# An attention and gated feed-forward block on one core: score and P·V half-steps regrouped in pairs of key blocks

## The chip, the cores and the metric

The kernel runs on one core of a Trainium2 chip. The metric is the device time in microseconds of one execution. Before the change three runs took 1682.72, 1683.56 and 1688.05 us; the median is 1683.56 us.

## What is computed

The reference is a transformer block with conditioned layer norms: 2048 rows of width 512, 32 query heads of width 16 on one shared key and value head, and a gated feed-forward part of inner width 1792.

```python
mod = (silu(c) @ w_mod).reshape(1, 6, 1, -1)          # sa, ca, ga, sb, cb, gb
h = layernorm(x) * (1 + ca) + sa
q, k, v = h @ wq (32 heads), h @ wk, h @ wv           # one k, one v for all heads
p = softmax(q k^T / 4)                                # per head, 2048 x 2048
x = x + ga * ((p v) @ wo)
h = layernorm(x) * (1 + cb) + sb
x = x + gb * ((sigmoid(h @ w_gate) * (h @ w_up)) @ w_down)
```

All products whose operands would lose too much in 16 bits are made of three passes with a high and a low part of each operand (`passes`, L470). P·V is done in float32.

## The kernel before

**Units and steps.** A prologue (the list `PLAN`, L38) makes the norms, k, v and the first q. Then a loop runs over 32 units (L1106): a unit is 256 query rows (`QU`) and 8 of the 32 heads. A unit has 16 steps `kb`, one for each block of 128 keys, and each step has two half-steps `n` (L1131). So there are 1024 half-steps.

**Halves of the array.** TensorE works as eight tiles of 64 rows by 32 columns: two halves by rows, called sides here, and four column strips. `columns` (L145) issues four matmuls, one for each strip of one side; they run together, since each has a tile of its own. A matmul's side follows from the partitions of its operands: partitions 0 to 63 are side 0, 64 to 127 side 1.

**What a half-step issues** is set by `ORDER` (L57): `a0, s0, c, a1, s1`, and then a piece of other work.
- `a` (`a_tile`, L603) is a tile of scores with queries on the partitions, into a bank `sa` (three banks). VectorE takes the maximum of each row (`a_max`, L597, line L136 in the profile, tile `mx`). These tiles run 84 ahead (`A0`), that is 21 steps.
- `s` (`st_tile`, L634) is a tile of scores with keys on the partitions, into a bank `st` (two banks); ScalarE takes its exponential into `P`.
- `c` (`pv`, L647) is P·V for a key block whose exponentials were made `LAG` = 2 steps ago: four matmuls of float32, one in each strip, each in two passes, so that eight show in the profile (`craw<-P,V`). They add to one PSUM bank `craw`, which both sides write in turn.

`sides(t)` (L578) gives the sides of the two half-steps of key block t: (0, 1) for even t and (1, 0) for odd t. In half-step `n` with `h = sides(kb)[n]`, the `a` and `s` tiles use side `1 - h`. `pv` uses side `sides(t)[n]` of its own key block `t = kb - 2`, which is as even or odd as `kb`.

**Turns.** When P·V passes from one side to the other, `hand_over` (L159) puts a tiny matmul behind the last one of the old side (`craw<-nought` in the profile), which counts up a semaphore, and `take_over` (L169) makes TensorE's queue wait for that count before the first P·V of the new side. Before the change `pv` hands over after the first half-step of each key block and takes over in its second.

**Pieces.** `piece` (L1095) puts a share of another product at the end of a half-step: q, the output projection (`po`), gate and up (`pgu`), down (`pd`), or a transposition (`pt`). Such a product is a `Couple` (L191) of two groups: each of its terms is a `columns` call on the side that P·V does not use and then one on the side that it does. `plan` and `places` (L1034, L1070) spread a group's terms over half-steps by rates (`RATE` 2.2 terms, fewer for some). `Transposes` (L785) are placed whole, and `split_evac` (L353) then writes the high and the low part of the norm's result: ScalarE scales it, VectorE casts the high part (`h2h`), GpSimd subtracts for the low part (`h2l`).

**Maxima.** When the last `a` tile of a unit is made (`n == 62`, L600), the next step gathers the maxima (`max_end`, L608, VectorE), its second half-step transposes them on TensorE and copies them on ScalarE (`max_rows`), and behind the first half-step of the step after that VectorE makes their low part and SyncE issues four small DMAs into two rows of the unit's `qp` tile (`low`, `qp<-mh`). The unit's `s` matmuls read these rows.

**Order.** All work of TensorE, VectorE and ScalarE in the loop is kept in the order of the program (`Ordered`, L130). After the loop, outside that order, come the last P·V, the last output projections and the last quarter of the feed-forward part (L1157 to L1191), with matmuls of 128 by 128.

Of the kernel before, what the change touches and what calls it, by code (L numbers as in the profile page):

```python
# [9 lines left out]
F32 = mybir.dt.float32  # L10
AF = mybir.ActivationFunctionType
ALU = mybir.AluOpType
# [4 lines left out]
P = 128  # L17
# [38 lines left out]
A0 = 84  # L56
ORDER = "a0", "s0", "c", "a1", "s1"  # L57
LAG = 2
# [31 lines left out]
def adaln_mqa_glu_kernel(  # L90
# [39 lines left out]
    class Ordered:  # L130
        def __init__(self, engine):
            self.engine = engine
# [36 lines left out]
    def take_over(since=None):  # L169
        pe.wait_ge(turn, done[0] if since is None else since)  # L170
# [20 lines left out]
    class Couple:  # L191
# [3 lines left out]
        def part(self, n0, n1):  # L195
            if n0 == 0:
                for g in self.gs:
                    g.open()
            m = self.gs[0].n
            for n in range(n0, n1):  # L200
                if n == m:
                    take_over(self.since)
                for j in (1 - side[0], side[0]):
                    g = self.gs[j ^ (n >= m)]
                    l_, r_, *cut = g.term(n % m, slice(64 * j, 64 * j + 64))
                    columns(cut[0](g.bank) if cut else g.bank, l_, r_, n == 0, n == 2 * m - 1)
                if n == m - 1:
                    self.since = None
                    if open_[0]:
                        hand_over()  # L210
                        self.since = done[0]
            if n1 == self.n:
                for k, g in enumerate(self.gs):
                    g.end(g.bank, k == 1)
# [138 lines left out]
    def split_evac(src, k, sc, sh, hi, lo):  # L353
        h32 = t32("h32")[:, :QU]
        act.activation(h32, src, AF.Identity, scale=sc[:, k:k + 1], bias=sh[:, k:k + 1])
        dve.tensor_copy(hi, h32)  # L356
        pool.tensor_tensor(lo, h32, hi, op=ALU.subtract)  # L357


# [216 lines left out]


    def sides(t):  # L578
        return (0, 1) if t % 2 == 0 else (1, 0)

    def spot(n):
        return n // 16, n // 8 % 2, n % 2, n // 2 % 4
# [14 lines left out]
    def a_max(i, n, sa):  # L597
        kc, qt, j, r = spot(n)
        dve.tensor_reduce(mxs[i][:, 4 * j + r, qt, kc:kc + 1], sa, axis=AX.X, op=ALU.max)
        if i > 0 and n == 62:  # L600
            pend.append((i,))

    def a_tile(i, n):  # L603
        a_max(*a_product(i, n))

    pend = []

    def max_end(i):  # L608
        m16 = wp.tile([64, 32], F32, tag="m16", name="m16", bufs=4)
# [24 lines left out]
    def st_tile(i, t, pr, j, second):  # L634
        qp = get_q(i)
        if not second:
            P_[pr] = P2.tile([P, 2, 512], F32, tag=f"P{pr}", name=f"P{pr}", bufs=PBUFS)
        p_ = P_[pr]
        s_ = sbank("st")
        columns(s_, kp[64 * j:64 * j + 64, t * P:(t + 1) * P], qp[64 * j:64 * j + 64, 2 * pr:2 * pr + 2].rearrange("p r q -> p (r q)"),  # L640
                True, True)
        act.activation(p_[:, j], s_, AF.Exp, scale=0.25)
        Ps[i, t, 2 * j + pr] = p_[:, j]
# [3 lines left out]
    def pv(i, t, second):  # L647
        c_ = raw_c["c"]
        side[0] = j = sides(t)[second]
        rs = slice(64 * j, 64 * j + 64)  # L650
        start, stop = t == 0 and not second, t == NKB - 1 and second
        if second:
            take_over()
        for hh in range(4):
            z = pe.matmul(c_[32 * hh:32 * hh + 32, :], V[rs, t, :], Ps[i, t, hh][rs, :], start=start, stop=stop)
            if start and hh == 0 and i > 0:
                behind(z, raw_c["out"])
        open_[0] = not stop
        if not second:
            hand_over()  # L660
        raw_c["last"] = z
        if second:
            for hh in range(4):
                del Ps[i, t, hh]
            if stop:
                unit_end(i)
# [118 lines left out]
    class Transposes:  # L785
        stage, n = "tr", 4

        def __init__(self, part, u):
            self.part, self.u = part, u

        def alone(self):
            self.part(0, 4)
# [1 line left out]
    def ffn_groups(b):  # L794
# [57 lines left out]
        def tr_part(u, z, n0, n1):  # L852
            if n0 == 0:
                pts2[z] = bank("pt2")
            pt = pts2[z]
            for n in range(n0, n1):
                k, t = 2 * z + n // 2, 2 * u + n % 2
                pe.transpose(pt[:, n * P:(n + 1) * P], x1[t][1][:, k * P:(k + 1) * P], ident)
            if n1 == 4:
                for k in range(2 * z, 2 * z + 2):  # L860
                    if u == 0:
                        h2[k] = t16("h2h"), t16("h2l")
                    split_evac(pt[:, k % 2 * QU:(k % 2 + 1) * QU], k, mods[4], mods[3],
                               *(h_[:, u * QU:(u + 1) * QU] for h_ in h2[k]))
# [82 lines left out]
            return Group("dn", 3 * n_, "pd", term, end)  # L947

        wos = [wo_group(t) for t in range(4)]
        trs = [Transposes(lambda n0, n1, u=u, z=z: tr_part(u, z, n0, n1), u) for z in range(2) for u in range(2)]  # L950
        gs = []
        at = len(uses) - NFC
        es = [Couple(gu_half(p, 0, 0, p), gu_half(p, 1, 0, p)) for p in range(0, ahead, 2)]
# [116 lines left out]
    def plan(s, hb):  # L1070
        if run:
            return
        g = pick(s)
        if g is None:
            lead[0] = 0.0
            return
        if g.stage == "tr":
            sizes = [4]
        else:
            q = g.stage == "q" and s < FIRST  # L1080
            light = not q and g.stage == "gu" and s < 2 * NU * NKB + SKIP
            rate, most = (QRATE, 1) if q else (ERATE, 2) if light else (RATE, MOST)
            sizes = []
            for leg in range(2):
                sizes += places(g.n // 2, hb + len(sizes), rate, most, (3 if leg == 0 else 0) if q else 0 if light else None, g.w)
            if hb + len(sizes) > 2 * len(units) * NKB:
                spare.insert(0, g)
                return
        at = 0
        for z in sizes:  # L1090
            run.append((g, at, at + z))
            at += z
        assert at == g.n, (at, g.n, g.stage)

    def piece(s, h):  # L1095
        plan(s, 2 * s + h)
        if run:
            g, n0, n1 = run.pop(0)
            if n1 > n0:
                g.part(n0, n1)  # L1100
# [5 lines left out]
    for i, (b, o) in enumerate(units):  # L1106
        if o == 0 and b == NQ - 1:
            ends = ffn_groups(NB - 1)
            first_rows.append(Couple(*ends[0][:2]))
        if o == 0 and b % 2 == 1 and b < NQ - 1:  # L1110
            blocks[b // 2] = ffn_groups(b // 2)
            wos, trs, _, es = blocks[b // 2]
            main.extend([*ready(b // 2, [Couple(*wos[:2]), trs[0], trs[2]], i), (None, len(es)), *ready(b // 2, es, i)])
        if o == 0 and b % 2 == 0 and b > 0:
            wos, trs, gs, _ = blocks.pop(b // 2 - 1)
            gs = [Couple(*wos[2:]), trs[1], trs[3], *gs]
            main.extend([*ready(b // 2 - 1, gs[:-KEPT], i), (None, KEPT), *ready(b // 2 - 1, gs[-KEPT:], i)])
        for kb in range(NKB):
            s = i * NKB + kb
            now[0] = s  # L1120
            if kb == NKB - QLEAD - 5 and i + 2 < len(units):
                get_q(i + 2)
            late, pend[:] = pend[:], []
            for z in [z for z in waits if z[0] <= s]:
                waits.remove(z)
                z[1]()
            rows = [max_end(*z) for z in late]
            an = A0 + 4 * s

            old, lows[:] = lows[:], []  # L1130
            for n, h in enumerate(sides(kb)):  # L1131
                for z in ORDER:
                    k = int(z[1:] or 0)
                    if z[0] == "a" and an + 2 * k + 1 - h < len(alist):
                        a_tile(*alist[an + 2 * k + 1 - h])
                    if z == "c" and len(vq) >= LAG:
                        pv(*vq[0], n == 1)
                    if z[0] == "s":
                        st_tile(i, kb, k, 1 - h, n == 1)
                if n == 1:  # L1140
                    lows.extend(z() for z in rows)
                piece(s, n)
                if n == 0:
                    for z in old:
                        z()
            if len(vq) >= LAG:
                vq.pop(0)
            vq.append((i, kb))
            while wdone < nw:
                if wdone < nw - 4 and (wdone + 0.5) * WSTEPS > (s + 1) * (nw - 4):  # L1150
                    break
                if wdone >= nw - 4 and s < WLAST + 3 * (wdone - nw + 4):
                    break
                wjobs[wdone]()
                wdone += 1
    assert wdone == nw and len(qdone) == 4 * NB
    while run:  # L1157
        piece(s, 1)
    while vq:
        for n in range(2):  # L1160
            pv(*vq[0], n == 1)
        vq.pop(0)
    while waits:
        now[0] += 1
        for z in [z for z in waits if z[0] <= now[0]]:
# [54 lines left out]
```

## Time and profile before

| | |
|---|---|
| median of three runs | 1683.56 us |
| the profiled execution's own time | 1685.55 us |
| its span, first to last instruction | 1683.7 us |
| TensorE (PE) busy | 1644.5 us, 98% |
| VectorE (DVE) busy | 1430.9 us, 85% |
| ScalarE (ACT) busy | 1295.4 us, 77% |
| GpSimd (POOL) busy | 610.5 us, 36% |
| mean granted TensorE clock | 0.99 |

PE's busy time counts a matmul from its start to its modelled end, and matmuls of different tiles and of the same pipeline overlap, so 98% does not say that the array is full. A row of a timeline gives start, length, engine, line, operation, tiles and count; neighbours of one kind are put together. `64*32` is the tile of the array that a matmul uses. L136 is a helper: everything that passes through `Ordered` has this line, so groups are told apart by their tiles.

### The profile page before, as it was taken

Reading aid. Unit: us, or ns where it says so; the run is one execution under the profiler, and the core shown is the slowest. Engines: PE = TensorE matmul, PEld = TensorE weight load, DVE = VectorE, ACT = ScalarE, POOL = GpSimd, SP = SyncE. Lnnn points to the kernel's source line nnn. Section 1 sums busy time; section 2 is a strip of 40 time slices with the busy share of each in tenths; the row PEclk is TensorE's granted clock in tenths of the full one; section 3 lists DMA queues with packets and bytes.
Section 4 is the critical chain, followed back from the end, with each engine's and each line's share of the span. In section 5 each row is a group of like instructions: output and inputs, shape, how many; then the busy total and the mean of one; then the engine's idle time right before and its main releaser. Section 6 shows DMA issues by size and latency. Waiting matters only on the chain.

```text
span 1683.7 us, 87854 instructions
## 1 busy us (share of the span) xinstructions
PE 1644.5 (98%) x39747; PEld 974.6 (58%) x39747; DVE 1430.9 (85%) x2428; ACT 1295.4 (77%) x2335; POOL 610.5 (36%) x784
## 2 busy tenths in 40 slices
PE   6999999999999999999999999999999999999998
PEld 3335445454456666666656666666666666654443
DVE  7789999999999999999999999999999999912311
ACT  5548889888888888888888888888888888884100
POOL 4432445475033442222543232223543333132423
PEclk9989999999999999999999999999999999999999
DMA  7111333331011120101021110100121110011211
GB/s 242 57 62 28 103 114 96 98 96 40 21 61 41 57 70 15 41 28 28 28 77 53 47 45 15 41 24 27 38 78 49 45 53 16 24 47 52 88 51 38
DMA packets 86722, 94.05 MB, mean 56 GB/s; under 512 B 24916, under 2 KB 65868, under 8 KB 86348
## 3 DMA queue, kind: packets, MB, share of 16 engines
q1 hardware_dynamic: 86348, 88.44, 17.0%
q8 instruction: 311, 5.10, 1.2%
q14 instruction: 63, 0.52, 0.1%
HBM read 67.82 MB, written 16.24 MB: 50 GB/s over the span
## 4 chain that ended last, share of the span: by engine, by line
PE 83%; DVE 11%; ACT 2%; issue 1%; DMA 1%; POOL 0%; SPq 0%; POOLq 0%; ACTq 0%; DVEq 0%
PE craw L136 23%; PE sa L136 16%; PE pgu L136 14%; PE st L136 10%; DVE mx L136 9%; PE pd L136 6%; PE pgu L187 5%; PE pd L187 3%; PE po L136 2%; PE pq L136 2%; ACT P L136 1%; DMA xall<-in_A_x_dram 1%; ACT th L136 1%; DVE h2h L136 1%; DVE st L136 1%
## 5 line engine op out<-in xcount | busy, mean ns | idle before, releaser
L136 DVE TENSOR_REDUCE mx<-sa 128x1 f32<-128x512 f32 x2048 | 1291.5, 682 | 64.0 <-PE sa L136 29.1
L136 ACT ACTIVATE P<-st 128x512 f32<-128x512 f32 x2048 | 1175.2, 598 | 197.2 <-PE st L136 133.6
L136 PE MATMUL craw<-P,V 64*32 64x512 f32 x8192 | 1088.0, 598 | 0.2
L136 PE MATMUL sa<-kp,qp 64*32 64x512 f16 (+1 forms) x7940 | 826.6, 378 | 10.5 <-DVE mx L136 9.8
L136 PE MATMUL st<-qp,kp 64*32 64x512 f16 x8192 | 831.8, 379 | 4.8 <-ACT P L136 4.5
L136 PEld LDWEIGHTS <-kp 64*32 64x32 f16 x8192 | 323.9, 91 | 254.5 <-issue 102.2
L136 PEld LDWEIGHTS <-qp 64*32 64x32 f16 (+1 forms) x7940 | 284.4, 92 | 166.5 <-issue 82.4
L136 PE MATMUL pgu<-h2h,gw 64*32 64x512 f16 x5248 | 273.8, 376 | 1.0
L136 PEld LDWEIGHTS <-gw 64*32 64x32 f16 x7872 | 175.0, 92 | 59.4 <-issue 16.2
L136 PEld LDWEIGHTS craw<-P,V 64*32 64x32 f32 x8192 | 184.5, 105 | 15.0 <-issue 2.0
L136 PE MATMUL pgu<-h2l,gw 64*32 64x512 f16 x2624 | 165.3, 376 | 0.3 <-POOL h2l L357 0.3
L901 POOL TENSOR_SCALAR th<-th 128x512 f32<-128x512 f32 x41 | 25.4, 620 | 356.0 <-ACT th L136 300.2
L136 PE MATMUL craw<-nought 64*32 64x1 f16 x571 | 93.1, 163 | 0.0
L557 POOL MEMSET qp<- 32x1024 f16 x60 | 56.7, 945 | 83.3 <-PE st L136 80.8
L321 POOL TENSOR_SCALAR wst<-wst 128x512 f32<-128x512 f32 x46 | 28.5, 621 | 144.7 <-DMA wst<-in_B_w_up_dram 89.4
L187 PE MATMUL pgu<-h2h,gw 128*128 128x512 f16 x240 | 71.9, 379 | 1.5 <-DVE h2h L356 1.5
L136 PEld LDWEIGHTS <-nought 64*32 64x32 f16 x571 | 53.1, 93 | 34.2 <-issue 28.8
L895 ACT ACTIVATE th<-pgu 128x512 f32<-128x512 f32 x15 | 9.0, 597 | 82.1 <-PE pgu L187 82.1
L136 PE MATMUL pd<-wdh,gh 64*32 64x512 f16 x1152 | 70.4, 376 | 0.6 <-DVE t L136 0.2
L136 PE MATMUL pd<-wdl,gh 64*32 64x512 f16 x1152 | 70.3, 376 | 0.0
L136 PE MATMUL pd<-wdh,gl 64*32 64x512 f16 x1152 | 69.7, 376 | 0.0
L136 DVE COPY u<-pgu 128x512 f32<-128x512 f32 x41 | 28.0, 682 | 48.6 <-PE pgu L136 48.4
(160 smaller groups left out, 1426.8 us busy)
## 6 DMA issues: line engine op xcount, KB each, us to landing
gw<-wD SPq DMA_DIRECT2D x56, 512.0 KB
wD<-gw SPq DMA_DIRECT2D x14, 512.0 KB
wm<-in_w_mod_dram SPq DMA_DIRECT2D x6, 1024.0 KB
qp<-qD SPq DMA_DIRECT2D x192, 32.0 KB
qD<-q SPq DMA_DIRECT2D x16, 256.0 KB
xr<-in_A_x_dram SPq DMA_DIRECT2D x16, 256.0 KB
out_dram<-ot SPq DMA_DIRECT2D x16, 256.0 KB
raw<-cs SPq DMA_DIRECT2D x248, 16.0 KB
```

The lines of the kernel that those rows point to most:

```text
L136: return (lambda *a, **k: keep(f_(*a, **k))) if pinned else f_
L187: pe.matmul(cut[0](self.bank) if cut else self.bank, l_, r_, start=(n == 0), stop=(n == self.n - 1))
L321: pool.tensor_scalar(w_, w_, SW, 0.0, op0=ALU.mult, op1=ALU.add)
L557: eng.memset(qp[j:j + 32], 0.0)
L895: act.activation(th, p_, AF.Tanh, scale=0.5 / (SH * SW))
L901: pool.tensor_scalar(th, th, 1.0, 1.0, op0=ALU.add, op1=ALU.mult)
```

## The change

- **Steps by twos.** `sides(t)` now changes with `t // 2`. Two steps belong together. In the even step of such a pair both half-steps do the first side of both key blocks of the pair, in the odd step the second side of both. P·V is done for the two key blocks of the previous pair, `vq[0]` and `vq[1]`.
- **Turns.** `pv` takes over only at the second side of an even key block, and hands over only behind the first side of an odd one (and at a unit's start).
- **Maxima.** The end of a unit's maxima is found by counting 64 tiles (`seen`); the gathering, the transposition and the DMAs come in the step after, the first half-step of the next one, and behind its second half-step.
- **h2's high part** is written by GpSimd instead of VectorE.
- **An empty half-step** follows the second of the two transpositions of each 256 rows (`sizes` is `[4, 0]`).
- `Couple` notes the count of turns at its middle and asserts that there was one since.

```diff
     def split_evac(src, k, sc, sh, hi, lo):
-        dve.tensor_copy(hi, h32)
+        pool.tensor_scalar(hi, h32, 1.0, 0.0, op0=ALU.mult, op1=ALU.add)
         pool.tensor_tensor(lo, h32, hi, op=ALU.subtract)
...
     def sides(t):
-        return (0, 1) if t % 2 == 0 else (1, 0)
+        return (0, 1) if t // 2 % 2 == 0 else (1, 0)
...
-        if i > 0 and n == 62:
+        seen[i] = seen.get(i, 0) + 1
+        if i > 0 and seen[i] == 64:
             pend.append((i,))
...
     def pv(i, t, second):
         side[0] = j = sides(t)[second]
-        if second:
+        if second and t % 2 == 0:
             take_over()
...
-        if not second:
+        if start or not second and t % 2 == 1:
             hand_over()
...
         if g.stage == "tr":
-            sizes = [4]
+            sizes = [*g.sizes]
...
-            rows = [max_end(*z) for z in late]
-            an = A0 + 4 * s
-            old, lows[:] = lows[:], []
-            for n, h in enumerate(sides(kb)):
+            ready_rows, rows[:] = rows[:], [max_end(*z) for z in late]
+            an = A0 + 4 * (s - kb % 2)
+            second = kb % 2 == 1
+            h = sides(kb)[second]
+            for n in range(2):
+                t = kb - kb % 2 + n
                 for z in ORDER:
                     k = int(z[1:] or 0)
-                    if z[0] == "a" and an + 2 * k + 1 - h < len(alist):
-                        a_tile(*alist[an + 2 * k + 1 - h])
-                    if z == "c" and len(vq) >= LAG:
-                        pv(*vq[0], n == 1)
+                    if z[0] == "a" and an + 4 * n + 2 * k + 1 - h < len(alist):
+                        a_tile(*alist[an + 4 * n + 2 * k + 1 - h])
+                    if z == "c" and vq:
+                        pv(*vq[n], second)
                     if z[0] == "s":
-                        st_tile(i, kb, k, 1 - h, n == 1)
-                if n == 1:
-                    lows.extend(z() for z in rows)
-                piece(s, n)
-                if n == 0:
-                    for z in old:
+                        st_tile(i, t, k, 1 - h, second)
+                if n == 0:
+                    lows[:] = [z() for z in ready_rows]
+                piece(s, n)
+                if n == 1:
+                    for z in lows:
                         z()
-            if len(vq) >= LAG:
-                vq.pop(0)
-            vq.append((i, kb))
+            if second:
+                vq[:] = [(i, kb - 1), (i, kb)]
```

More of the change, by code (lines that the diff above doesn't have):

```diff
@@ L201, in part @@
                 if n == m:
+                    assert self.since is not None or done[0] > self.marks
                     take_over(self.since)
@@ L207, in part @@
                 if n == m - 1:
-                    self.since = None
+                    self.since, self.marks = None, done[0]
                     if open_[0]:
@@ L604, in a_tile @@
         a_max(*a_product(i, n))
-    pend = []
+    pend, seen = [], {}
     def max_end(i):
@@ L636, in st_tile @@
         if not second:
-            P_[pr] = P2.tile([P, 2, 512], F32, tag=f"P{pr}", name=f"P{pr}", bufs=PBUFS)
-        p_ = P_[pr]
+            P_[t % 2, pr] = P2.tile([P, 2, 512], F32, tag=f"P{pr}", name=f"P{pr}", bufs=PBUFS)
+        p_ = P_[t % 2, pr]
         s_ = sbank("st")
@@ L786, in adaln_mqa_glu_kernel, with __init__ @@
         stage, n = "tr", 4
-        def __init__(self, part, u):
-            self.part, self.u = part, u
+        def __init__(self, part, u, sizes):
+            self.part, self.u, self.sizes = part, u, sizes
         def alone(self):
@@ L949, in ffn_groups @@
         wos = [wo_group(t) for t in range(4)]
-        trs = [Transposes(lambda n0, n1, u=u, z=z: tr_part(u, z, n0, n1), u) for z in range(2) for u in range(2)]
+        trs = [Transposes(lambda n0, n1, u=u, z=z: tr_part(u, z, n0, n1), u, ([4], [4, 0])[z]) for z in range(2) for u in range(2)]
         gs = []
@@ L1158, in adaln_mqa_glu_kernel @@
         piece(s, 1)
[L1159 to L1162, printed above, removed]
+    for n in range(4):
+        pv(*vq[n % 2], n > 1)
     while waits:
```

## The prediction

> **What bounds the kernel now.** First the span, then the chain of work that ended last, then the groups of the loop.
>
> ```profile
> span 1683.7 us, 87854 instructions
> PE 83%; DVE 11%; ACT 2%; issue 1%; DMA 1%; POOL 0%; SPq 0%; POOLq 0%; ACTq 0%; DVEq 0%
> ```
> ```profile
> L136 DVE TENSOR_REDUCE mx<-sa 128x1 f32<-128x512 f32 x2048 | 1291.5, 682 | 64.0 <-PE sa L136 29.1 <-PE st L136 11.6 <-PE craw L136 0.9
> L136 ACT ACTIVATE P<-st 128x512 f32<-128x512 f32 x2048 | 1175.2, 598 | 197.2 <-PE st L136 133.6 <-PE sa L136 10.5 <-ACT P L136 0.3
> L136 PE MATMUL craw<-P,V 64*32 64x512 f32 x8192 | 1088.0, 598 | 0.2
> L136 PE MATMUL st<-qp,kp 64*32 64x512 f16 x8192 | 831.8, 379 | 4.8 <-ACT P L136 4.5
> L136 PE MATMUL sa<-kp,qp 64*32 64x512 f16 x7856 | 800.8, 378 | 4.2 <-DVE mx L136 3.5
> ```
>
> TensorE carries 83% of the chain, and VectorE is close behind it: 1291.5 us of maxima over 2048 tiles are 0.63 us each, so a half-step with two of them cannot last under 1.26 us. How a half-step fits into that is seen in the timeline of TensorE:
>
> ```profile
> 802.12 0.40 PE L136 MATMUL sa<-kp,qp 64*32 64x512 f16 x4
> 802.14 0.64 PE L136 MATMUL craw<-P,V 64*32 64x512 f32 x4
> 802.33 0.40 PE L136 MATMUL st<-qp,kp 64*32 64x512 f16 x4
> 802.55 0.40 PE L136 MATMUL sa<-kp,qp 64*32 64x512 f16 x4
> 802.60 0.61 PE L136 MATMUL craw<-P,V 64*32 64x512 f32 x4
> 802.76 0.40 PE L136 MATMUL st<-qp,kp 64*32 64x512 f16 x4
> ...
> 803.04 0.16 PE L136 MATMUL craw<-nought 64*32 64x1 f16 x1
> ```
>
> Two things are to be seen. Matmuls of one side follow each other: sa, st, sa, st start 0.21 us apart, so a slot of one side is 0.214 us (0.64 / 3). And P·V, on the other side, runs **beside** them: its two passes begin at 802.14 and 802.60, and at 803.04 the tile is free. Four slots of scores (0.86) and P·V (0.90; 0.86 where it does not begin behind a turn, by the 0.43 of the pass at 1530.27 below) hide each other. The kernel lives on this.
>
> **The change, part by part: the sides.** I write down which side each half-step uses. Before, `a` and `s` use `1 - h` with `h = sides(kb)[n]`, and P·V uses `sides(kb - 2)[n]`, which is `h`, since `kb` and `kb - 2` are alike in `t % 2`. After, `sides` goes by `t // 2 % 2`. Scores use `1 - h` with `h = sides(kb)[second]`; P·V is for the pair before, whose `t // 2` differs by one. Its `sides` are the other way round, so it uses `1 - h` too.
>
> ```
> half-step            1  2  3  4 | 5  6  7  8
> before, scores       1  0  0  1 | 1  0  0  1
> before, P·V          0  1  1  0 | 0  1  1  0
> after, scores        1  1  0  0 | 0  0  1  1
> after, P·V           1  1  0  0 | 0  0  1  1
> ```
>
> This is the core of my forecast: after the change scores and P·V of a half-step stand on the **same side** and cannot hide each other; the other side is idle but for pieces. A half-step costs 4 x 0.214 + 0.86 = 1.72 us and its pieces, where it cost 0.86 and its pieces. That is over the 1.26 us of VectorE and twice ScalarE's 0.57 (1175.2 / 2048), so TensorE alone sets the pace.
>
> How many terms have the pieces? The loop's weight loads for them:
>
> ```profile
> L136 PEld LDWEIGHTS <-gw 64*32 64x32 f16 x7872 | 175.0, 92 | 59.4 <-issue 16.2 <-PE craw L136 1.7
> L136 PEld LDWEIGHTS <-gh 64*32 64x32 f16 x2304 | 54.1, 92 | 16.7 <-issue 4.2
> L136 PEld LDWEIGHTS <-gl 64*32 64x32 f16 x1152 | 29.3, 92 | 7.3
> L136 PEld LDWEIGHTS <-a 64*32 64x32 f16 x1344 | 30.2, 92 | 9.9 <-issue 2.0 <-POOL a L713 0.7
> L136 PEld LDWEIGHTS <-wdh 64*32 64x32 f16 x640 | 14.4, 93 | 2.7 <-issue 0.6 <-PE craw L136 0.6
> L136 PEld LDWEIGHTS <-wdl 64*32 64x32 f16 x320 | 7.2, 94 | 1.5 <-issue 0.6
> ```
>
> 13,632 in all, eight to a term: 1704 terms, 1.664 for each of 1024 half-steps. A term takes one slot of both sides.
>
> **The turns.** By the table a side now changes once in four half-steps, 256 times. What overlaps there depends on how far TensorE looks past a matmul whose tile is busy.
>
> ```profile
> 1530.27 0.61 PE L136 MATMUL craw<-P,V 64*32 64x512 f32 x4
> 1530.34 0.40 PE L136 MATMUL pgu<-h2l,gw 64*32 64x512 f16 x4
> 1530.55 0.40 PE L136 MATMUL pgu<-h2h,gw 64*32 64x512 f16 x4
> 1530.70 0.16 PE L136 MATMUL craw<-nought 64*32 64x1 f16 x1
> 1530.71 0.40 PE L136 MATMUL pgu<-h2l,gw 64*32 64x512 f16 x4
> ...
> 1530.98 0.64 PE L136 MATMUL craw<-P,V 64*32 64x512 f32 x4
> ```
> ```profile
> 107.84 0.72 PE L136 MATMUL sa<-kp,qp 64*32 64x512 f16 x8
> ```
> ```profile
> 108.24 0.64 PE L136 MATMUL st<-qp,kp 64*32 64x512 f16 x4
> 108.66 0.64 PE L136 MATMUL sa<-kp,qp 64*32 64x512 f16 x4
> 109.09 1.10 PE L136 MATMUL st<-qp,kp 64*32 64x512 f16 x8
> ```
>
> The program has a piece's terms as side, other side, side, other side; yet the second term of the free side starts at 1530.55, before the first of the busy one (1530.71). At 107.84 eight matmuls run at once: the first `a` tile of the first half-step, and that of the second, on the other side, which stands behind twelve matmuls (108.24, 108.66, 109.09) that start later. So the queue looks at least twelve matmuls ahead. At a turn P·V of the new side waits for the nought of the old one: 1530.70 to 1530.98, 0.28 us, is the least. With all else done ahead the next P·V comes 0.28 us after the old one ends; with only twelve matmuls of sight the pieces' last terms, `a0` and `s0` come behind it, three slots, 0.64 us. I take 0.40, nearer to the first, because twelve is only what the trace happens to show.
>
> The Trainium skill says otherwise in "TensorE: Matmul & The Clock Gate", part 3 on packing small matmuls: matmuls start and end strictly in program order. The rows above speak against it (P·V at 802.14 starts before the `s` tile of 802.33 that precedes it in the program); what the strict order would give is a rival below.
>
> **The sum.** A pair has four P·V, 0.90 + 3 x 0.86 = 3.48; three gaps on one side, each with four slots of scores and 1.664 of terms, 3 x 5.664 x 0.214 = 3.64; and one turn, 0.40. That is 7.52 us; 256 pairs are 1925. `a` tiles end 42 half-steps early: less 0.75 x 42 x 2 x 0.214 = 13. For what the sum leaves out (transpositions, the maxima's small matmuls, the half clock at the start, the projections between the last P·V) I add 30, a guess. The loop takes 1942 us. It begins at 108.2 and now ends here:
>
> ```profile
> 1538.84 1.06 PE L136 MATMUL craw<-P,V 64*32 64x512 f32 x8
> ```
>
> so 1683.7 - 1539.9 = 143.8 us of tail stay. In the tail GpSimd takes over eight casts behind which TensorE waits:
>
> ```profile
> L713 POOL TENSOR_SCALAR a<-raw 128x256 f16<-128x256 f32 x31 | 12.6, 408 | 2.6
> L136 DVE CAST h2h<-h 128x256 f16<-128x256 f32 x24 | 13.7, 604 | 1.9 <-ACT h L136 1.8
> ```
>
> 8 x 0.41 = 3 us, if none of it hides. In the loop the same move costs nothing: GpSimd is busy 36% of the span, the empty half-step gives it time, and VectorE's 14 us are saved where it no longer decides. That half-step holds no matmul and moves pieces only. Span: 108 + 1942 + 144 + 3 = 2197; the profiled execution took 1685.55, 1.9 more than its span, and the median of the runs is 2.0 below that. **2197 us.**
>
> **The maxima.** The last DMAs into `qp` move from the middle of step 12 to the end of step 13, two steps before they are read.
>
> ```profile
> 792.06 3.00 SPq L136 DMA_DIRECT2D qp<-mh  x4
> ```
>
> Two steps of 3.76 us are 7.5, issuing takes 3.0, and 4.5 remain for landing. SP has nothing else at that place. I cost it at nothing; if they landed 1 us late in each of 31 units, 31 us, inside the range.
>
> **The clock.** TensorE's clock could fall when half the array idles.
>
> ```profile
> 110.58:113.99 3.41, 3.41 (x52) 0.50 0.02 5
> 113.99:117.41 3.42, 3.42 (x73) 0.50 0.00 0
> ...
> 1537.35:1540.76 3.41, 2.54 (x26) 1.00 0.00 0
> 1540.77:1544.17 3.40, 3.40 (x8) 0.50 0.00 0
> ```
>
> Columns are the stretch, its length, PE's busy time, the granted clock. From 110.58 to 113.99 matmuls ran without a break, nearly all on one side, and the clock stayed at half in the next stretch; in 1537.35 to 1540.76 P·V ran alone on one side for about two thirds of the time, and the clock fell to half behind it. So it seems to count used array, not busy time. After the change a pair uses (4 x 0.86 x 0.5 + 16 x 0.214 x 0.5 + 4 x 1.664 x 0.214) / 7.52 = 0.65 of the array, and 0.5 without pieces; the stretch that fell had about 0.33. I expect full clock, without certainty. The Trainium skill ("TensorE: Matmul & The Clock Gate", part 1) lets the clock fall after an idle stretch only; by it too the clock stays.
>
> **The rivals.**
> - *Strict order at the turns.* Only one slot overlaps: the turn is 5.664 x 0.214 - 0.214 = 1.0 instead of 0.40, 256 x 0.60 = 154 more: 2351 us. The skill's rule in part 3 is this. Against it: the rows at 1530 and 107. Chance 0.08.
> - *The clock falls* in each stretch that one side fills alone, one of 3.4 us in a pair at half speed: 256 x 1.7 = 435 more, 2632 us; half clock throughout would be some 4100. For it: the row at 1537. Chance 0.12.
> - *Faster: the sides stay opposite*, the table above being wrong. Then P·V stays hidden, half of the 512 turns go, and VectorE loses 14 us of casts. A turn shows 0.04 to 0.28 us; at 0.05 they give 13 us, so up to 27 less: about 1660 to 1680, say 1670 us. It decides at one place: whether `sides` of the pair before equals `sides` of this one. Against it: the parity. Chance 0.04.
>
> **How the numbers follow.** Forecast 0.71, rivals 0.08, 0.12 and 0.04, something else and slower 0.05. The forecast's own range runs from 2150 (turn 0.28: 31 less; P·V at two full passes of 0.42: 16 less) to 2290 (turn 0.64: 61 more; late maxima 31). To hold 8 in 10 it reaches to the strict order: 2145 to 2370. Faster by over 0.3% (5 us, about what a measurement tells from no change) 0.04, same 0.01, slower 0.95.
>
> **What would show it.** In the timeline craw and sa or st start one after the other, never within 0.1 us, in most half-steps; the loop's pairs last 7.5 us; VectorE and ScalarE wait for PE sa and PE st over 0.4 us in every half-step, and their busy shares fall to about 65% and 59%. The nought count falls from 571 to about 350. From nought to the next craw 0.3 to 0.6 us say that the sight is deep, 1.0 that the order is strict. A granted clock under 0.95 shows the clock rival. If craw still starts beside sa, the table is wrong and with it everything.

## The result, and the profile after

| | before | after |
|---|---|---|
| median of four runs each (lowest to highest) | 1683.14 us (1682.58 to 1688.05) | 2266.17 us (2245.05 to 2268.65) |
| profiled execution, its span | 1685.55 us, 1683.7 us | 2266.40 us, 2264.5 us |
| VectorE / ScalarE busy | 85% / 77% | 66% / 58% |

The changed kernel takes 1.343 times as long, 95% interval 1.334 to 1.351. The forecast was 2197 us: the sign, the cause and the range (2145 to 2370) hold, and the time is 70 us too low. The runs of the changed kernel differ with the clock that TensorE was granted: the one of 2245.05 us has a mean clock of 0.995, the profiled one 0.985. One run of e6 below took 5567.38 us, and two runs of the kernel before, taken beside the experiments, 5993.35 and 4653.69 us; no median or ratio here rests on them.

From the page of the changed kernel, the span, the busy times, the granted clock in 40 slices and the chain by engine:

```profile
span 2264.5 us, 87862 instructions
PE 2234.6 (99%) x39688; PEld 1054.9 (47%) x39688; DVE 1500.3 (66%) x2396; ACT 1309.9 (58%) x2335; POOL 622.4 (27%) x818
PEclk8896999999999999999999999999999999999999
PE 95%; DVE 3%; issue 1%; ACT 1%; DMA 0%; POOL 0%; SPq 0%; POOLq 0%; ACTq 0%; DVEq 0%
```

VectorE's part of the chain falls from 11% to 3%; TensorE alone sets the pace. The groups of the loop (busy time, mean ns of one, idle time before them and what ended it):

```profile
L136 DVE TENSOR_REDUCE mx<-sa 128x1 f32<-128x512 f32 x2048 | 1377.3, 688 | 566.2 <-PE sa L136 513.0
L136 ACT ACTIVATE P<-st 128x512 f32<-128x512 f32 x2048 | 1186.2, 596 | 757.6 <-PE st L136 648.6
L136 PE MATMUL craw<-P,V 64*32 64x512 f32 x8192 | 1078.6, 594 | 1.2
L136 PE MATMUL sa<-kp,qp 64*32 64x512 f16 (+1 forms) x7940 | 792.5, 381 | 6.3 <-DVE mx L136 6.2
L136 PE MATMUL st<-qp,kp 64*32 64x512 f16 x8192 | 785.6, 380 | 1.3 <-ACT P L136 1.3
L136 PEld LDWEIGHTS <-gw 64*32 64x32 f16 x8064 | 213.7, 91 | 99.2 <-issue 21.8
```

Each matmul is as long as before (594 ns against 598 for P·V, 381 and 380 against 378 and 379). What grew is waiting: VectorE's idle time behind sa went from 29.1 to 513.0 us, ScalarE's behind st from 133.6 to 648.6. So nothing on TensorE became slower; matmuls that ran beside each other now run one after the other. One full half-step and the turn behind it, in the timeline of TensorE:

```profile
1001.33 0.41 PE L136 MATMUL sa<-kp,qp 64*32 64x512 f16 x4
1001.55 0.41 PE L136 MATMUL st<-qp,kp 64*32 64x512 f16 x4
1001.77 0.41 PE L136 MATMUL pgu<-h2h,gw 64*32 64x512 f16 x4
1001.98 0.41 PE L136 MATMUL pgu<-h2l,gw 64*32 64x512 f16 x4
1002.20 0.41 PE L136 MATMUL sa<-kp,qp 64*32 64x512 f16 x4
1002.41 0.41 PE L136 MATMUL st<-qp,kp 64*32 64x512 f16 x4
1002.63 1.02 PE L136 MATMUL craw<-P,V 64*32 64x512 f32 x7
1003.07 0.40 PE L136 MATMUL pgu<-h2h,gw 64*32 64x512 f16 x4
1003.09 0.59 PE L136 MATMUL craw<-P,V 64*32 64x512 f32 x1
1003.49 0.16 PE L136 MATMUL craw<-nought 64*32 64x1 f16 x1
...
1003.50 0.40 PE L136 MATMUL pgu<-h2h,gw 64*32 64x512 f16 x4
...
1004.16 0.59 PE L136 MATMUL craw<-P,V 64*32 64x512 f32 x3
```

From 1001.33 to 1002.63 six tiles of one side start 0.21 us apart: the old half-step's second scores, two terms, the new one's first scores. P·V waits for all of them, because it needs the same side, and while it runs only one piece of the other side (1003.07) goes beside it. The tile of the craw of 1003.09 is free at 1003.52 (its 0.59 us less the 0.16 that the nought of a single column takes), and the next P·V, on the other side, starts at 1004.16: a turn of 0.64 us.

I put all 1024 P·V of the trace in order and took their lengths and the gaps between them; with the loop's ends this gives the whole difference:

| term | forecast | measured | difference |
|---|---|---|---|
| P·V, 1024 | 891 | 914 | +23 |
| gaps on one side, 768 | 932 | 930 | -2 |
| turns, 256 | 102 | 163.5 | +61 |
| guess of 30, a tiles that end early -13; measured, the first half-steps ahead of any P·V | 17 | 9 | -8 |
| start of the loop | 108.2 | 110.9 | +3 |
| tail with the casts | 147 | 137 | -10 |
| span | 2197 | 2264.5 | +67 |

About 15 us of the measured side, by an estimate made below, are a stretch at half clock. The count of turns is as foreseen, about 350 (571 before):

```profile
L136 PE MATMUL craw<-nought 64*32 64x1 f16 x344 | 56.2, 163 | 0.0
```

### The profile page after: what moved, and what is told of

Read it like the earlier page. It is cut to its first block, busy times and chain, and to the rows that moved or that the text cites. A ratio compares the mean times of both kernels' runs of the same rounds, so it can differ in the third digit from the quotient of the medians.

```text
span 2264.5 us, 87862 instructions
## 1 busy us (share of the span) xinstructions
PE 2234.6 (99%) x39688; PEld 1054.9 (47%) x39688; DVE 1500.3 (66%) x2396; ACT 1309.9 (58%) x2335; POOL 622.4 (27%) x818
## 4 chain that ended last, share of the span: by engine, by line
PE 95%; DVE 3%; issue 1%; ACT 1%; DMA 0%; POOL 0%; SPq 0%; POOLq 0%; ACTq 0%; DVEq 0%
PE craw L136 31%; PE sa L136 20%; PE st L136 16%; PE pgu L136 11%; PE pd L136 5%; PE pgu L187 3%; PE pd L187 2%; PE pq L136 2%; PE po L136 2%; DVE mx L136 2%; PE pt L136 0%; DMA xall<-in_A_x_dram 0%; PE pmod L136 0%; DVE st L136 0%; PE pk L136 0%
## 5 line engine op out<-in xcount | busy, mean ns | idle before, releaser
L136 DVE TENSOR_REDUCE mx<-sa 128x1 f32<-128x512 f32 x2048 | 1377.3, 688 | 566.2 <-PE sa L136 513.0
L136 ACT ACTIVATE P<-st 128x512 f32<-128x512 f32 x2048 | 1186.2, 596 | 757.6 <-PE st L136 648.6
L136 PE MATMUL st<-qp,kp 64*32 64x512 f16 x8192 | 785.6, 380 | 1.3 <-ACT P L136 1.3
L136 PE MATMUL pgu<-h2h,gw 64*32 64x512 f16 x5376 | 477.2, 380 | 0.1
L136 PEld LDWEIGHTS <-kp 64*32 64x32 f16 x8192 | 260.5, 93 | 339.0 <-issue 256.4
L136 PEld LDWEIGHTS craw<-P,V 64*32 64x32 f32 x8192 | 271.2, 107 | 155.0 <-PE craw L136 6.4
L136 PE MATMUL pgu<-h2l,gw 64*32 64x512 f16 x2688 | 266.0, 380 | 0.0
L136 PE MATMUL pd<-wdh,gh 64*32 64x512 f16 x1152 | 115.3, 380 | 0.0
L136 PE MATMUL po<-woh,a 64*32 64x512 f16 x896 | 82.1, 380 | 0.0
L136 PEld LDWEIGHTS <-gh 64*32 64x32 f16 x2304 | 63.5, 91 | 27.9 <-issue 4.3
L910 POOL TENSOR_TENSOR gl<-th,gh 128x512 f16<-128x512 f32 x56 | 65.0, 1160 | 4.7
```

The lines of the kernel that those rows point to most:

```text
L136: return (lambda *a, **k: keep(f_(*a, **k))) if pinned else f_
L910: pool.tensor_tensor(lo[:, to], th[:, of], hi[:, to], op=ALU.subtract)
```

## The experiments

**e1: the scores on the other side.** All of the change stays; `a` and `s` tiles use side `h` instead of `1 - h`.

```diff
-  if z[0] == "a" and an + 4 * n + 2 * k + 1 - h < len(alist):
-      a_tile(*alist[an + 4 * n + 2 * k + 1 - h])
+  if z[0] == "a" and an + 4 * n + 2 * k + h < len(alist):
+      a_tile(*alist[an + 4 * n + 2 * k + h])
...
-      st_tile(i, t, k, 1 - h, second)
+      st_tile(i, t, k, h, second)
```

> The changed kernel with one thing undone: the score tiles use side h instead of 1 - h, so that they stand opposite to P·V again; all else is as changed. Theory 'same side': the whole loss is that scores and P·V share a side, so this is near the kernel before, 1655 to 1690 us, and craw starts within 0.1 us of sa or st. Rival 'grouping': the loss comes from taking steps by twos as such (turns, waits for exponentials), wherever the sides are: 2150 us or more.

Measured: 1666.54 us (1663.68 to 1668.65), 0.9894 of the kernel before (0.9878 to 0.9911). Span, busy times and chain from its page, and its timeline of TensorE:

```profile
span 1664.9 us, 87820 instructions
PE 1623.7 (98%) x39688; PEld 966.0 (58%) x39688; DVE 1415.6 (85%) x2396; ACT 1292.3 (78%) x2335; POOL 622.2 (37%) x818
PE 86%; DVE 8%; ACT 3%; issue 1%; DMA 1%; SPq 1%; POOL 0%; POOLq 0%; ACTq 0%; DVEq 0%
```
```profile
801.36 0.42 PE L136 MATMUL sa<-kp,qp 64*32 64x512 f16 x4
801.41 0.64 PE L136 MATMUL craw<-P,V 64*32 64x512 f32 x4
801.57 0.42 PE L136 MATMUL st<-qp,kp 64*32 64x512 f16 x4
801.79 0.42 PE L136 MATMUL sa<-kp,qp 64*32 64x512 f16 x4
801.86 0.61 PE L136 MATMUL craw<-P,V 64*32 64x512 f32 x4
```

P·V starts at 801.41 beside the sa tile of 801.36 again. The same matmuls (39688 on TensorE in both), with nothing but their side changed, take 600 us less. The loss is the side, all of it, and the other parts of the change are worth about 18 us of gain.

**e2: the kernel before, with its scores moved to P·V's side.** The same edit the other way, in the kernel without the change: sides turn 512 times, not 256.

```diff
-  if z[0] == "a" and an + 2 * k + 1 - h < len(alist):
-      a_tile(*alist[an + 2 * k + 1 - h])
+  if z[0] == "a" and an + 2 * k + h < len(alist):
+      a_tile(*alist[an + 2 * k + h])
...
-      st_tile(i, kb, k, 1 - h, n == 1)
+      st_tile(i, kb, k, h, n == 1)
```

> The kernel before with only the score tiles moved to side h, that is onto P·V's side; steps, turns and all else as before. Theory 'same side' with a sight of twelve matmuls: in two half-steps two P·V of 0.88, one gap on the same side of 1.21 (304 us over 256 in the changed kernel) and one turn of 0.64 (164 over 256), 3.61 us, 512 times, 1848, with 116 ahead of the first P·V and 144 of tail: 2110 us, less than the changed kernel, since it turns twice as often and each turn lets the sides overlap. With strict order the turn is 1.0 and the time 2290. Rival 'grouping': no grouping, so about 1685 us.

Measured: 2106.18 us (2103.38 to 2107.63), ratio 1.2504 (1.2484 to 1.2523). A turn in its timeline of TensorE:

```profile
801.97 1.03 PE L136 MATMUL craw<-P,V 64*32 64x512 f32 x8
802.46 0.40 PE L136 MATMUL pd<-wdh,gh 64*32 64x512 f16 x4
...
802.83 0.16 PE L136 MATMUL craw<-nought 64*32 64x1 f16 x1
...
802.85 0.40 PE L136 MATMUL pd<-wdl,gh 64*32 64x512 f16 x4
...
803.50 0.59 PE L136 MATMUL craw<-P,V 64*32 64x512 f32 x1
```

The same side costs over 400 us in a kernel that has none of the change. It is faster than the changed kernel, because at a turn the scores of the new half-step stand on the free side and overlap: it has twice the turns (512, mean 0.62 us), and each takes the place of a gap of 1.2 us. In both kernels the length of a turn goes by the terms of the piece in it (medians at full clock, us):

```
terms in the piece                    0     1     2     3
changed kernel, turn               0.28  0.45  0.67  0.88
e2, turn                           0.28  0.45  0.67  0.88
changed kernel, gap on one side    0.84  1.06  1.28  1.50
strict order at a turn, worked out 0.64  0.86  1.07  1.28
```

The last row has the four score tiles and the terms, one slot each, less the one slot that overlaps. e2 lies 180 us under its time by strict order, and at its time by a sight of twelve matmuls (2110).

**e3: P·V last in the half-step,** so that fewer matmuls of the busy side stand ahead of the new side's.

```diff
-ORDER = "a0", "s0", "c", "a1", "s1"
+ORDER = "a0", "s0", "a1", "s1", "c"
```

> The changed kernel with P·V last in each half-step (a0, s0, a1, s1, c). Theory 'sight of twelve matmuls': the turn of 0.64 us is long because the new side's a0 and s0 stand behind more than twelve matmuls that still wait; with P·V last only its second pass and the pieces stand between, so the new side's score tiles run ahead and the turn falls to 0.28 to 0.45 us: 50 to 90 us less, 2175 to 2215 us. Rival: the 0.64 us is a fixed cost of the semaphore and the first weight loads; then the turns stay at 0.64 and the time at about 2265.

Measured: 2240.87 us (2239.30 to 2242.29), ratio 1.3303 (1.3280 to 1.3326); against the changed kernel's run at about the same clock (2245.05), 4 us. A miss: its turns have a mean of 0.61 us (medians 0.33, 0.33, 0.58 and 1.02 with 0, 1, 2 and 3 terms). I had forgotten that the new side has its own `a1` and `s1` ahead of its P·V too: four slots and the terms, where the old P·V covers four slots. By this account, made after the fact, a turn takes at least one slot for each term (0, 0.21, 0.43, 0.64); the medians lie 0.12 to 0.37 above that, and what makes up the rest is open. So e3 says nothing on the depth of the queue's sight.

**e5: the terms of the free side ahead of those of the busy one,** in the changed kernel: within a piece, all terms of one side and then all of the other.

```diff
-            for n in range(n0, n1):
...
-                for j in (1 - side[0], side[0]):
+            for j in (1 - side[0], side[0]):
+                for n in range(n0, n1):
```

> The changed kernel with a piece's terms in another order: all its matmuls on the side without P·V first, then all on the other, in place of one by one. The changed kernel's turns took 0.28, 0.45, 0.67 and 0.88 us where the piece in them had 0, 1, 2 and 3 terms. Theory 'sight of twelve matmuls': in the new order the free side's terms stand behind fewer waiting matmuls and run ahead, so with 2 terms the turn falls to 0.45 and with 3 to 0.67, 181 turns by 0.215 us, 39 us less than the changed kernel at like clock (about 2207 us, or 2227 with a stretch at half clock). Rival 'strict order' or a cost that goes with the number of terms: no change.

Measured: 2248.62 us (2237.23 to 2280.90), ratio 1.3333 (1.3284 to 1.3383). At a clock of 0.995 it takes 2237.23 against 2245.05. Turns with 0 and 1 terms are unchanged (0.28, 0.45); with two they fall from 0.67 to 0.57, where 0.45 was expected, with three from 0.88 to 0.80, where 0.67 was. All turns together take 150 us instead of 164. Right direction, a fifth of the size in the time.

**e6: e5's order in e1.** The edits of e1 and e5 together.

> e1 (scores opposite to P·V) with the order of e5. Here both sides are full, so at most the turns shrink a little: 0 to 10 us less than e1's 1666.5. If TensorE's turns do not decide where VectorE sets the pace, no change within 3 us.

Measured: 1672.03 us, the median of five runs (1670.89 to 1674.91), ratio 0.9934 (0.9918 to 0.9950), where e1 has 0.9894. A miss of some 6 us in the other direction; why is open.

**e4: e1 with the cast back on VectorE.**

```diff
-        pool.tensor_scalar(hi, h32, 1.0, 0.0, op0=ALU.mult, op1=ALU.add)
+        dve.tensor_copy(hi, h32)
```

> e1 with h2's high part back on VectorE. If the move to GpSimd saves VectorE's time where VectorE sets the pace, this is up to 14 us (24 casts of 0.60 us) slower than e1; if GpSimd's part in the tail costs more, it is up to 3 us faster; within 3 us of e1 if neither decides.

Measured: 1674.35 us (1671.07 to 1678.89), ratio 0.9942 (0.9926 to 0.9958). So the change with opposite sides and without its cast (steps by twos, the empty half-step, the later maxima) brings about 10 us, and the cast on GpSimd another 8.

**e7: e1 without the empty half-step.**

```diff
-  ..., u, ([4], [4, 0])[z]) for z in range(2) for u in range(2)]
+  ..., u, ([4], [4])[z]) for z in range(2) for u in range(2)]
```

> e1 without the empty half-step behind the second transposition. If GpSimd's two passes over h2 delay the first gate matmuls, TensorE waits for h2l at three blocks' starts and this is 1 to 6 us slower than e1; otherwise equal within 3 us.

Measured: 1671.58 us (1669.46 to 1671.82), ratio 0.9925 (0.9911 to 0.9939): some 5 us more than e1, with intervals that touch.

**e8: the kernel before with only the cast on GpSimd** (the diff of e4 backwards).

> The kernel before with h2's high part on GpSimd alone. e4 against e1 gave 8 us for this move where steps go by twos. If it is VectorE's time that is saved, it is the same here: 4 to 12 us less than before. If it only pays with the empty half-step, the first gate matmuls wait for GpSimd and it is within 3 us of before or slower.

Measured: 1680.84 us (1677.16 to 1685.01), ratio 0.9984 (0.9971 to 0.9996), about 3 us. So the cast is worth 3 us here and 8 us in e1. One reading is that the rest comes only where the half-step behind it is empty, which hides a wait for GpSimd; that is argued from e7 and e8, not shown, since no run has steps by twos with the cast on VectorE and without the empty half-step.

**e9: q's copy out of PSUM on VectorE,** in the changed kernel. In the profiled run of that kernel the clock falls behind a stall that two such copies on ScalarE make; this takes them off ScalarE.

```diff
-        act.activation(q32, pq, AF.Identity, scale=1.0 / (SH * SW))
+        dve.tensor_scalar(q32, pq, 1.0 / (SH * SW), None, op0=ALU.mult)
```

> The changed kernel with q's copy out of PSUM on VectorE, which is idle a third of the time, instead of ScalarE. Theory 'clock': in the profiled run of the changed kernel two such copies delayed the exponentials at 178 us, TensorE waited 0.9 us, a 3.4 us stretch used 0.37 of the array and the clock stayed at half for 34 us, some 17 to 20 us of time; without the copies there no stretch falls, all runs have a mean clock of 0.99 or more and 2235 to 2247 us. Rival: the falls of the clock come by chance or from elsewhere: runs at 0.982 to 0.986 and 2255 to 2270 us are among them as before.

Measured: 2253.19 us at a mean clock of 0.991, and five runs of 2299.00 to 2302.08 us at 0.968 to 0.971. The expectation failed: its profiled run has its own fall to half clock, at 270.4 us for 6.8 us, and the other five were at half for longer still. So the falls do not depend on those copies alone.

**e10: the changed kernel again,** unaltered, beside e9.

> The changed kernel again on the chip of e9, as its measure: by either theory some runs at a mean clock of 0.98 and about 2266 us and some at 0.995 and about 2245 us, each hundredth of the clock being worth about 20 us.

Measured: 2267.92 us (2246.63 to 2297.21), ratio 1.3424 (1.3381 to 1.3468). The run of 2297.21 us is the profiled one. Its span and clock, and four of its stretches (PE busy, weight loads, VectorE, ScalarE, GpSimd, granted clock, DMA):

```profile
span 2295.3 us, 87862 instructions
PEclk9855999999999999999999999999999999999999
```
```profile
97.49:100.90 3.41, 2.56 (x11) 0.73 (x11) 2.98 (x6) 1.55 (x4) 1.09 (x1) 1.00 0.20 66
158.97:162.38 3.41, 3.41 (x45) 1.11 (x41) 1.36 (x3) 1.17 (x3) 0.00 (x0) 0.50 0.00 0
217.00:220.41 3.41, 3.41 (x48) 1.27 (x44) 0.95 (x2) 1.53 (x3) 0.00 (x0) 0.50 0.00 0
220.41:223.83 3.42, 3.42 (x69) 1.57 (x61) 1.76 (x4) 1.55 (x3) 0.00 (x0) 1.00 0.06 14
```

The clock falls at 100.95, ahead of the loop, and stays at half until 220.41, 119.5 us, although TensorE is busy without a break from 107.8 on. In the changed kernel's first profile the loop has 13.7 and 34.1 us at half. So 71.7 us more at half go with a span 30.8 us longer: 0.43 us for each, an estimate from these two executions.

## Why the prediction was right in its cause and 70 us low

**The sides: right.** After the change "scores and P·V of a half-step stand on the **same side**". e1 and e2 show it from both ends: the side alone takes the changed kernel to 1666.54 us, and the kernel before to 2106.18. The price of the faster rival was right as well: had the table been wrong, 1670 us was forecast, and e1, which makes it wrong, takes 1666.54.

**Slots, terms, P·V: right in size.** Gaps on one side sum to 930 us for a forecast of 932. P·V takes 0.883 us at full clock; I had 0.87.

**The maxima: right at nothing.** The matmuls of `st`, which read `qp`, waited 1.3 us in the whole execution (their row above), for a bank and not for a DMA; and the gaps on one side, where a late `qp` would show, are 2 us under the forecast. The casts in the tail and the guess of 30 are together 18 us too dear, about 5 of it because 24 more terms of gate and up run in the loop and not in the tail (8064 weight loads for 7872).

**The turns: the step that failed.** "I take 0.40, nearer to the first, because twelve is only what the trace happens to show." It is 0.64, the other bound, and 61 of the 67 us. That the rest agrees to 6 us is partly luck: P·V (+23) and the tail with the guess (-18) cancel.

The medians by terms say why a sight of about twelve matmuls is no accident of one place. While P·V's second pass runs, the nought and the old side's `a1` and `s1` wait, nine matmuls. With no terms the new side's scores are seen past them, and only the 0.28 of the hand-over remain. One term on the busy side makes thirteen, one more than the queue saw past at 107.84: the new scores are not seen and take two slots afterwards, 0.45. With two and three terms the later free terms are hidden too: one slot more for each, 0.67 and 0.88. Most turns have two. While P·V's first pass runs, the four matmuls of its second pass wait as well, thirteen again, and nothing of the new side starts: its first matmul comes beside the second pass, as in the row of 1003.07 (medians 0.02 to 0.08 us behind that pass's start, over 236 turns).

I had both bounds and their rows, and did not count what waits at a turn of the changed kernel. The 0.28 stood at 1530.70, in the kernel before, where the new scores are on the side that P·V leaves, so that none of them had to slip by; the twelve stood at 107.84. A bound that the trace shows holds for what stood in the queue there: count the same for the new order before leaning to it.

**How far that is settled.** Twelve, with the nought counted, fits the eight medians of two kernels. It does not fit e5: with the free terms first, two terms should have given 0.45 and gave 0.57. So TensorE starts matmuls past waiting ones, only so far; the exact rule (a count of matmuls, of weight loads among them, or of something else) stays open.

**Strict order: refuted.** By it a turn with no terms would take 0.64 instead of 0.28, and e2 would take 2290 us instead of 2106. The Trainium skill ("TensorE: Matmul & The Clock Gate", part 3) says that matmuls keep the program's order at start and end, "strict FIFO, no reordering"; the turns of this case speak against it, where the matmuls use different tiles of the array.

**The clock: expected full, and wrong for a stretch.** In the changed kernel's first profile (columns as above):

```profile
177.98:181.39 3.41, 2.69 (x41) 1.05 (x36) 2.21 (x4) 3.06 (x6) 2.33 (x4) 1.00 0.09 21
181.39:184.80 3.41, 3.41 (x32) 1.24 (x27) 1.38 (x2) 1.20 (x2) 1.96 (x3) 0.50 0.44 120
...
212.10:215.50 3.40, 3.40 (x41) 0.89 (x37) 1.38 (x2) 1.19 (x3) 1.81 (x3) 0.50 0.00 0
215.50:218.90 3.40, 3.40 (x56) 1.25 (x52) 2.48 (x4) 2.07 (x4) 0.00 (x0) 1.00 0.02 5
```

It falls behind the stretch at 177.98, in which TensorE is busy for 2.69 of 3.41 us, and comes back at 215.5: 34.1 us, at 0.43 about 15 us of the span. The stall inside the stretch of 177.98, in ScalarE's timeline and in TensorE's:

```profile
178.38 1.08 ACT L136 ACTIVATE q<-pq 128x512 f32<-128x512 f32 x2
179.34 1.71 ACT L136 ACTIVATE P<-st 128x512 f32<-128x512 f32 x3
```
```profile
178.91 0.39 PE L136 MATMUL sa<-kp,qp 64*32 64x512 f16 x4
180.01 0.40 PE L136 MATMUL st<-qp,kp 64*32 64x512 f16 x4 [0.71 <-ACT P L136]
```

Two copies of q delay the exponentials, and TensorE waits 0.71 us for a bank. That this stall makes the fall is not shown: a like stall at 283.8 us (0.62 us, behind two copies of q too) leaves the clock alone, and e9, without those copies, falls elsewhere. Where it falls, and why runs differ, stays open. In the rival's form (each stretch on one side falls, 2632 us) it did not come.

## What to carry to other kernels

Where two streams hide each other on two halves of the array, write down for every step which half each uses, before and after: a regrouping that shifts the period of one stream's sides against the lag of the other can put both on one half, and the whole second stream appears in the time (1.343 times here). The cure is one sign: e1, which keeps the rest of the change, is the fastest of these kernels at 0.9894 of the kernel before. And a queue that looks past a waiting instruction does so only for a few: count what waits ahead of the work that is to slip by.

## What the runs showed of the hardware

**The clock can stay at half while matmuls run without a break.** From the matmul records I worked out the used share of the array in stretches of 3.41 us (each matmul's length at its clock by its part of the array):

```
kernel   stretch          matmuls run  array used  clock, then
changed  177.99 - 181.40      0.74        0.37      full, half
changed  283.80 - 287.21      0.77        0.37      full, full
changed  188.23 - 212.12      1.00     0.50-0.70    half, half
changed  212.12 - 215.53      1.00        0.75      half, full
e10       97.53 - 100.95      0.47        0.35      full, half
e10      111.19 - 217.00      1.00     0.50-0.75    half, half
e10      217.00 - 220.41      1.00        0.73      half, full
```

In e10, 31 stretches in a row are full of matmuls and stay at half, and in the changed kernel's first profile the seven from 188.23 to 212.12; they use 0.50 to 0.75 of the array. At full clock every other stretch of both loops, over 500 in each, used 0.46 to 0.77 and stayed full. So in this kernel either clock tends to hold itself, and the time depends on where the falls come. The two stretches in the loop that used 0.37 ran matmuls for 0.74 and 0.77 of their time; one of e10 at 312.6 us ran them for 0.77 too but used 0.48, and the clock stayed. That the clock goes by the used share is argued from such rows, not shown. At the loop's start the clock falls in the kernel before too, and in the changed kernel's first profile; in both it was full again after 13.7 us, in e10 only after 119.5. No single threshold parts all these rows: 0.75 did not raise it at 158.97 in e10, and 0.73 did at 217.00. The Trainium skill ("TensorE: Matmul & The Clock Gate", part 1) has the full clock return after one busy window of about 3.4 us; 31 busy ones did not bring it back here.

**The hand-over between sides** costs about 0.28 us, from the end of one side's P·V to the start of the other's, where nothing else stands between, in the changed kernel and e2 alike; the shortest turn of the two takes 0.26 us.
